# Splitting the second output product of three tiles into two token halves, and turning batch 6's keys earlier

## The chip, the cores and the metric

The kernel runs on one core of a Trainium2 chip. The engines of the core work side by side, each through its own instructions in order: TensorE (PE, with its weight loads shown apart as PEld), VectorE (DVE), ScalarE (ACT), GpSimd (POOL) and SyncE (SP, which here only issues transfers). What one engine needs of another it waits for on semaphores. The metric is the device time of one execution in microseconds. It was 226.36 us before the change, the median of 3 runs.

## The reference

Attention with keys and values pooled eight to one, followed by a feed-forward layer whose hidden value is the largest of three linear maps. Cut to what is computed:

```python
# q, k, v: (8 batches, 8 heads, 576 tokens, 64)
k_p = k.reshape(B, H, 72, 8, D).mean(axis=3)
v_p = v.reshape(B, H, 72, 8, D).mean(axis=3)
attn = softmax(q @ k_p.T / 8)
x = (attn @ v_p)               # as 4608 tokens x 512
h = max(x @ w1, x @ w2, x @ w3)      # 4608 x 768
out = h @ w_out                # 4608 x 512
```

## The kernel before

The 4608 tokens are worked through as nine tiles of 512. Tile n has a hidden stage (`hidden`, the maximum of the three maps) and an output stage. The maximum of three is taken as x @ w1 plus max(0, x @ (w2 - w1), x @ (w3 - w1)), and the x @ w1 part is folded into the output: the output of a tile is x @ (w1 @ w_out) + h' @ w_out, a product over ten rows of 128 (four of x, six of h').

A batch has 576 tokens, a tile 512. So the attention of the batches runs beside the tiles, one batch ahead: while tile n is in its stages, batch n+1 is scored (`s0` to `s7`, one head each), then its five chunks of 128 tokens are summed over the values (`v0` to `v4`) and turned into the layout that the tiles read (`x0` to `x4`, transposes that SP issues as DMAs).

For tiles 2, 3 and 4 the output stage is seven products in place of eight: a two by two split of the matrix product by a scheme with seven multiplications (`out_seven`, `PRODUCTS`). Each of the seven works on 256 tokens (two halves of 128, called m = 0 and 1) by 256 output columns, with five row blocks r for each half: ten matmuls. The line that does them is L715. The products go into three PSUM banks: 1, 6, 5 and 3 into oA, 2 into oB, and 7 and then 4 into oC. The banks of these tiles come from two groups: oA has a tag `tr` with one buffer, so that each of its four products waits until the one before is copied out; oB and oC come from the tag `pw` with three buffers, which the hidden stages' products use too. `evict` takes the results out: ACT copies oA into an output buffer (L725), DVE adds oB or oC to it (L728). Product 2's bank is added to the half of the output that 1 and 6 wrote; oC is added to the upper columns of the other half when 5 and 7 are done, and after product 4 to the upper columns of the first half. Then SP stores each half.

In these tiles the order on every engine is written out by hand, as a list of steps (`MIDDLE`). `middle(n)` walks through that list and records each step's instructions, and the engines keep that order. A digit is a product; `v2 x2` are chunk 2's value sums, its normalization and its transpose; `7:T` is the transpose of batch 7's queries; `6:k` is the key turn of batch 6.

The value sums of a chunk are 8 matmuls (L270) into a buffer of the tag `att`, which has two and gives them in rotation. DVE then takes the reciprocal of the row sums (L276) and multiplies (L278); the multiply is the last reader of that buffer. The scores (`psc`, L220) and the key turn use the same two buffers.

The key turn (`turn_k`) is three transposes on PE (L201) of the pooled keys `kp` into a PSUM tile `pkt`, and four copies out of it into the key matrices `kz` (L210): two by DVE, then two by ACT. Scores of a batch read both matrices. In tiles 2 to 4 the turn of the batch that is to be scored stands in the hidden stage, behind its first product. Batch 6 is scored from the start of tile 5's hidden stage on, and its turn stands at the end of tile 4's output stage.

The hidden products of a tile are L364 (`pw`), their relu on ACT is L370, their maximum on DVE L372; the exponentials of the scores are L225 on ACT.

Of the kernel before, what the change touches and what calls it, by code (L numbers as in the profile page):

```python
# [14 lines left out]
def kernel(  # L15
# [46 lines left out]
    def psum(shape, dtype, name, tag, bufs):  # L62
        return pools[-1].tile(shape, dtype, name=name, tag=tag, bufs=bufs)
# [86 lines left out]
    def tokens(t0, t1, k0=0, k1=KCH):  # L150

        t0, t1 = t0 % RING, (t1 - 1) % RING + 1
        assert t0 < t1
        return xT[:, k0:k1, t0:t1]
# [244 lines left out]
    def new_two():  # L399
        return sb3.tile([128, 2, C], F32, name="osb", tag="osb", bufs=3)  # L400
# [160 lines left out]
    def turns(n):  # L561
        return (pad3 if n % 2 else pad)[:, 0:4]
# [17 lines left out]
    def out_w(z, r0, r1):  # L580

        i, j = divmod(z, 2)
        c = slice(HALF * i, HALF * i + HALF)
        return (wm_sb[:, 2 * j + r0:2 * j + r1, c] if r1 <= 2
                else wo_sb[:, JH * j + r0 - 2:JH * j + r1 - 2, c])

    def out_s(z):
        return so_new[0][:, z - 1]
# [56 lines left out]
    def out_seven(n):  # L645

        mid = len(pools) < 3
        if mid:
            o = {}
        else:  # L650
            o = sb2.tile([128, 2304], F32, name="ob", tag="et")[:, 0:2048].rearrange(
                "p (j m c) -> p j m c", j=2, m=2)
            o = [o[:, 0], o[:, 1]]
        lo, hi = slice(0, HALF), slice(HALF, C)
        banks, done = {}, set()

        def store(e, j, c):
            for u in range(2):
                b, g = divmod(2 * (4 * n + 2 * j) + u, NG)
                pair = g + 2 < NG and GS[g + 2] == GS[g] + 4  # L660
                for m in range(0, 2, 1 + pair):
                    b, g = divmod(2 * (4 * n + 2 * j + m) + u, NG)
                    dst = out[S * b:S * b + S, :].rearrange("(r g) c -> r g c", g=NG)
                    e.dma_start(out=dst[:, GS[g]:GS[g] + 4 * pair + 1:4, c],
                                in_=o[j][64 * u:64 * u + 64, m:m + 1 + pair, c])

        def bank(of, m):
            if n < LAST:
                if of not in banks:
                    if mid:  # L670
                        tag = TR if of == "A" else PW
                        banks[of] = psum([128, 2, HALF], F32, name=f"o{of}", tag=tag[0],
                                         bufs=tag[1])
                    elif of == "A":
                        banks["A"] = psum([128, 2, 2, HALF], F32, name="oA", tag="val",
                                          bufs=1)[:, 0]
                    else:
                        tag = (PO, SC)[of == "C"]
                        banks[of] = psum([128, 2, HALF], F32, name=f"o{of}", tag=tag[0],
                                         bufs=tag[1])  # L680
                return banks[of]
            if (of, m) not in banks:
                tag = {"A": PA, "B": SC, "C": BC if m == 0 else SC}[of]
                banks[of, m] = psum([128, 2, HALF], F32, name=f"o{of}", tag=tag[0],
                                    bufs=tag[1])[:, 0:1]
            return banks[of, m]

        def product(i, *ms):
            if mid:
                for r in range(5):  # L690
                    for m in ms:
                        matmuls(i, m, (r,))
            else:
                for m in ms:
                    matmuls(i, m)
            done.update((i, m) for m in ms)
            evict(i, ms)

        def matmuls(i, m, rows=range(5)):
            of = "B" if i == 2 else "C" if i in (4, 7) else "A"  # L700
            p = bank(of, m)[:, m if n < LAST else 0]
            za, zb = PRODUCTS[i]
            for r in rows:
                c = slice(128 * m, 128 * m + 128)
                if isinstance(zb, str):
                    z = int(zb[1]) - 1
                    left = (tt_all[0][:, z, r, c] if mid else
                            turns(n)[:, z, r, c] if r < 2 else th[n][z][:, r - 2, c])
                else:
                    at = HALF * (zb % 2) + 128 * m  # L710
                    left = (tokens(NB * n + at, NB * n + at + 128)[:, 2 * (zb // 2) + r] if r < 2
                            else hTs[n][:, JH * (zb // 2) + r - 2, at:at + 128])
                right = (out_s(int(za[1]))[:, r] if isinstance(za, str)
                         else out_w(za, r, r + 1)[:, 0])
                nc.tensor.matmul(  # L715
                    p, left, right, stop=(r == 4), skip_group_check=True,
                    start=(i in FIRST and r == 0 and (m == 0 or n == LAST)))

        def evict(i, ms):
            m, at = ms[0], slice(ms[0], ms[-1] + 1)  # L720

            def copy(j, c):
                if j not in range(len(o)):
                    o[j] = new_two()
                nc.scalar.copy(out=o[j][:, at, c], in_=bank("A", m))  # L725

            def plus(j, c, of):
                nc.vector.tensor_tensor(out=o[j][:, at, c], in0=o[j][:, at, c],  # L728
                                        in1=bank(of, m), op=ALU.add)

            def ended(*parts):
                return all((z, k) in done for z in parts for k in range(2))

            if i in (1, 5, 6, 3):
                copy(int(i in (5, 3)), lo if i in (1, 3) else hi)
            elif i == 2:
                plus(0, lo, "B")
            elif i == 4:
                plus(0, hi, "C")
            if i in (5, 7) and (12 - i, m) in done:  # L740
                plus(1, hi, "C")
            if n == LAST and i in (5, 7) and ended(5, 7):
                store(nc.sync, 1, hi)
            if n == LAST and i == 3 and ended(3):
                store(nc.scalar, 1, lo)
            if n < LAST and i in (5, 7, 3) and ended(5, 7, 3):
                store(nc.sync, 1, slice(0, C))
            if n == LAST and i in (2, 4) and ended(i):
                store((nc.gpsimd, nc.sync)[i // 4], 0, (lo, hi)[i // 4])
            if n < LAST and i in (2, 4) and ended(2, 4):  # L750
                store(nc.sync, 0, slice(0, C))

        return product
# [102 lines left out]
    def weave():  # L856

        products, seen = {}, {}
        for name in ORDER.split():
# [29 lines left out]
        2: """  # L889
            h k k5< q5< v5< h a1 a3 a2 a4 S S ! v3+2 h h s0 h s1 h s2 h s3 h s4 b1 f f ! k4+1 h s5  # L890
            h s6 h s7 h b2 b3 b4 ! k4+2 v4+1
            1 v0 x0 2 v1 x1 6 7 v2 x2 5:T 5 v3 x3 v4 x4 3 4
        """,
        3: """
            h k k6< q6< v6< h a1 a3 a2 a4 f ! v4+2 h h s0 h s1 h s2 h s3 h s4 b1 f ! k5+1 h s5
            h s6 h s7 h b2 b3 b4 ! k5+2 v5+1
            1 v0 x0 2 v1 x1 6:T 6 7 v2 x2 5 v3 x3 v4 x4 3 4
        """,
        4: """
            h k k7< q7< v7< h a1 a3 a2 a4 f ! v5+2 h h s0 h s1 h s2 h s3 h s4 b1 f ! k6+1 h s5  # L900
            h s6 h s7 h b2 b3 b4 f ! k6+2 v6+1
            1 v0 x0 2 v1 x1 7:T 6 7 v2 x2 5 v3 x3 v4 x4 3 6:k 4 v6+2 k7+3 v7+3
        """}
    folds = iter([f for wi in range(1, 3) for f in [fold_w(wi)] * 4])

    def middle(n):

        pieces, outs, out_tiles = hidden(n), None, project(n)
        for name in MIDDLE[n].split():
            if name == "h":  # L910
                next(pieces)
            elif name == "F":
                next(out_tiles)
            elif name == "f":
                next(next(folds))
            elif name == "!":
                held[:] = gate
            elif name.isdigit():
                outs = outs or out_seven(n)
                outs(int(name), 0, 1)  # L920
            elif name[0] in "ab":
                sums_of(n, name)
            elif name[2:3] in ("<", "+"):
                pool_step(n, name)
            else:
                b, _, step = name.rpartition(":")
                do(int(b or n + 1), step)
        assert next(pieces, None) is None

    tt_all.append(const.tile([128, 4, 5, HALF], F16, name="tt", tag="tt"))  # L930
    for n in range(1, 5):
        middle(n)
# [12 lines left out]
    outs = out_seven(LAST)  # L945
# [36 lines left out]
```

## Time and profile before

| | us |
|---|---|
| runs before the change | 226.1, 226.36, 226.71 |
| profiled execution, time | 226.65 |
| profiled execution, span from first to last instruction | 224.9 |
| PE busy | 215.5 (96%) |
| DVE busy | 149.1 (66%) |
| POOL busy | 140.1 (62%) |
| ACT busy | 122.2 (54%) |
| output stage of tile 2 | 89.90 to 99.16 |
| output stage of tile 3 | 111.61 to 120.87 |
| output stage of tile 4, with the key turn | 133.32 to 143.29 |

How to read it: the profile is one execution, its times are microseconds from the first instruction. A row of the timeline gives start, duration, engine, line, operation, the tile written and the tiles read, the shape, the number of instructions merged into the row, and in brackets how long the engine had been idle before it and whom it waited for. The duration of a matmul row reaches to a modelled end and overlaps the next row, so that the time a group of matmuls costs PE is the distance between starts. The difference between the time of an execution and its span lies before the first and behind the last instruction.

### The profile page before, as it was taken

How to read it: one execution, taken by the hardware profiler on the slowest of the kernel's cores; microseconds unless marked ns; L12 is line 12 of the kernel's file. 1: busy time of each engine (PE TensorE's matmuls, PEld its weight loads, DVE VectorE, ACT ScalarE, POOL GpSimd, SP SyncE). 2: the span in 40 equal slices, each digit the busy share in tenths (PEclk: the TensorE clock that was granted, in tenths of full speed). 3: DMA queues.
4: the chain of work that ended last, by engine and by line, in shares of the span. 5: the costliest groups of instructions: out<-in, count | busy, mean ns of one | idle time of the engine just before them, and what ended most of it. 6: DMA issues, size and time to landing. Idle time of an engine off the chain costs nothing.

```text
span 224.9 us, 4690 instructions
## 1 busy us (share of the span) xinstructions
PE 215.5 (96%) x1806; PEld 146.9 (65%) x1807; DVE 149.1 (66%) x292; ACT 122.2 (54%) x221; POOL 140.1 (62%) x111
## 2 busy tenths in 40 slices
PE   7888999999999999999999999899999999999993
PEld 2477745558656545975596568555677777788882
DVE  4668876037594395877588668636677786898840
ACT  2277524755874578238724862484786446555330
POOL 7984300999949977787768757999600903772020
PEclk9999999999999999999999999999999999999999
DMA  6999999989749999659999998764341534200266
GB/s 176 210 196 197 204 208 205 206 151 236 137 105 174 233 200 224 121 108 159 244 202 158 161 261 140 153 155 92 71 95 36 122 63 89 47 3 0 60 201 163
DMA packets 50710, 33.54 MB, mean 149 GB/s; under 512 B 27040, under 2 KB 46368, under 8 KB 50688
## 3 DMA queue, kind: packets, MB, share of 16 engines
q0 software_dynamic: 20304, 16.98, 48.1%
q1 hardware_dynamic: 29936, 15.87, 31.9%
q10 hardware_dynamic: 448, 0.39, 0.7%
q8 instruction: 14, 0.23, 0.4%
q14 instruction: 8, 0.07, 0.1%
HBM read 34.60 MB, written 9.44 MB: 196 GB/s over the span
## 4 chain that ended last, share of the span: by engine, by line
PE 71%; DMA 12%; POOL 11%; issue 2%; DVE 1%; ACT 1%; POOLq 0%; ACTq 0%
PE pw L364 21%; PE oA L715 9%; DMA vt<-in_v_dram 8%; PE pA L791 7%; PE po L418 7%; PE po L414 5%; PE psc L220 4%; PE oC L715 4%; DMA mw<-in_moe_w_dram 4%; PE pC L791 3%; POOL half L163 3%; PE pav L270 3%; PE oB L715 2%; POOL half L164 2%; PE pB L791 2%
## 5 line engine op out<-in xcount | busy, mean ns | idle before, releaser
L364 PE MATMUL pw<-xT,mw 128*128 128x512 f16 (+1 forms) x336 | 72.8, 348 | 0.3 <-ACT xT L264 0.2
L364 PEld LDWEIGHTS <-mw 128*128 128x128 f16 x336 | 31.7, 98 | 20.4 <-issue 0.6
L372 DVE TENSOR_TENSOR hT<-t,pw 128x512 f16<-128x512 f16 (+1 forms) x42 | 25.4, 609 | 23.9 <-ACT et L225 14.9
L225 ACT ACTIVATE et<-psc 72x576 f16<-72x576 f32 (+2 forms) x54 | 35.2, 661 | 6.7 <-PE psc L220 6.6
L163 POOL TENSOR_TENSOR half<-vt 72x2048 f32<-72x2048 f16 x7 | 28.4, 4058 | 13.8 <-DMA vt<-in_v_dram 13.3
L164 POOL TENSOR_TENSOR half<-half 72x1024 f32<-72x1024 f32 (+1 forms) x13 | 27.3, 2098 | 10.7 <-DVE rcp L276 6.1
L370 ACT ACTIVATE t<-pw 128x512 f16<-128x512 f32 (+1 forms) x42 | 22.5, 537 | 14.8 <-PE pw L364 14.3
L278 DVE TENSOR_TENSOR xn<-pav,rcp 128x512 f16<-128x512 f32 x40 | 27.7, 691 | 1.4
L220 PE MATMUL psc<-qT,kz 128*128 128x320 bf16 (+2 forms) x120 | 22.6, 278 | 1.3 <-DVE qT L196 0.9
L418 PE MATMUL po<-mwo,hT 128*128 128x512 f16 (+1 forms) x102 | 23.5, 366 | 0.0
L220 PEld LDWEIGHTS <-kz 128*128 128x128 bf16 x143 | 13.1, 98 | 13.8 <-ACT qT L196 1.1
L163 POOL TENSOR_TENSOR half<-ktFalse 96x1536 f32<-96x1536 f16 x6 | 18.8, 3129 | 4.0 <-issue 2.9
L797 ACT CAST pad<-pA 128x512 f16<-128x512 f32 x27 | 15.6, 588 | 7.2 <-PE pA L791 7.0
L566 POOL TENSOR_TENSOR pad<-xT 128x256 f16<-128x256 f16 x8 | 6.0, 752 | 21.2 <-ACT pad L797 12.6
L270 PEld LDWEIGHTS <-et 72*128 72x128 f16 x320 | 15.2, 98 | 3.5 <-issue 0.2
L725 ACT COPY osb<-oA 128x512 f32<-128x512 f32 x12 | 7.0, 586 | 19.2 <-PE oA L715 19.2
L276 DVE RECIPROCAL rcp<-pav 128x8 f32<-128x8 f32 x40 | 8.1, 203 | 13.8 <-PE pav L270 13.3
L414 PE MATMUL po<-wm,xT 128*128 128x512 f16 (+1 forms) x68 | 16.6, 366 | 0.0
L270 PE MATMUL pav<-vp,et 72*128 72x65 f16 x320 | 16.4, 194 | 0.1
L423 ACT COPY osb<-po 128x512 f32<-128x512 f32 (+1 forms) x16 | 9.2, 573 | 12.0 <-PE po L418 12.0
L791 PEld LDWEIGHTS <-sw 128*128 128x128 f16 x144 | 13.7, 98 | 2.5
L768 DVE TENSOR_TENSOR pad<-pad,pC 128x512 f16<-128x512 f16 x18 | 12.3, 685 | 3.9 <-PE pC L791 3.6
(122 smaller groups left out, 383.2 us busy)
## 6 DMA issues: line engine op xcount, KB each, us to landing
out_dram<-osb SPq DMA_DIRECT2D x38, 128.0 KB, 5.3
ktFalse<-in_k_dram POOLq DMA_DIRECT2D x7, 576.0 KB, 8.3
qb<-in_q_dram POOLq DMA_DIRECT2D x7, 576.0 KB, 11.6
vt<-in_v_dram POOLq DMA_DIRECT2D x7, 576.0 KB, 16.8
mw<-in_moe_w_dram POOLq DMA_DIRECT2D x9, 256.0 KB, 9.3
out_dram<-osb SPq DMA_DIRECT2D x8, 256.0 KB, 5.7
ktTrue<-in_k_dram SPq DMA_DIRECT2D x3, 384.0 KB, 5.1
out_dram<-ob SPq DMA_DIRECT2D x8, 128.0 KB, 2.6
```

The costliest lines, as they stand in the source:

```text
L163: yield e.tensor_tensor(out=f, in0=t[:, :, 0:4, :], in1=t[:, :, 4:8, :], op=ALU.add)
L164: yield e.tensor_tensor(out=f[:, :, 0:2, :], in0=f[:, :, 0:2, :], in1=f[:, :, 2:4, :], op=ALU.add)
L220: nc.tensor.matmul(out, kz_all[b % 2][f % 2][rows, h, :], qTs[b][rows, n + i0:n + i1, 64 * (h % 2):64 * (h % 2) + 64], start=True, stop=True)
L225: nc.scalar.activation(out=out, in_=in_, func=FT.Exp, scale=1.0 / 64.0)
L270: nc.tensor.matmul(pav[:, h // 4, 65 * (h % 4):65 * (h % 4) + 65], ets[b][:, h, c0:c0 + 128], vp_all[:, b, h, :], start=True, stop=True)
L278: nc.vector.tensor_tensor(out=xn, in0=pv[:, :, :, 0:D], in1=rcp.to_broadcast([128, 2, 4, D]), op=ALU.mult)
L364: mm = nc.tensor.matmul(pw, w_sb[wi][:, kc, bass.ts(jc, 128)], x[:, kc], start=(kc == 0), stop=(kc == KCH - 1))
L372: nc.vector.tensor_tensor(out=hT[:, jc, c0:c1], in0=t, in1=pw, op=ALU.max)
L414: nc.tensor.matmul(po, tokens(128 * m, 128 * m + 128)[:, kc], wm_sb[:, kc, c], start=(kc == 0), stop=False)
L418: nc.tensor.matmul(po, hT[:, jc, bass.ts(mm, 128)], wo_sb[:, jc, c], start=False, stop=(jc == JCH - 1))
L715: nc.tensor.matmul(p, left, right, stop=(r == 4), skip_group_check=True, start=(i in FIRST and r == 0 and (m == 0 or n == LAST)))
L791: mm = nc.tensor.matmul(p[:, w], a[:, kc, bass.ts(g, 128)], b[:, kc, :], start=(i in FIRST and w + kc == 0), stop=(w + kc == 2), skip_grou ...
```

## The change

Two parts. Product 2 of tiles 2, 3 and 4 can now be written as two steps, `2l` (m = 0) and `2h` (m = 1), each with five matmuls, and its bank is added only when both are done. In tiles 2 and 3 the first half stays where product 2 stood and the second goes between `v3` and `v4`. In tile 4 the first half stands behind `v1`, the second behind `v4`, and the key turn of batch 6 stands behind that, ahead of products 3 and 4 (before, between 3 and 4). In the built program the number of instructions on each engine's work stays the same.

```diff
@@ out_seven, product
                 for m in ms:
                     matmuls(i, m)
             done.update((i, m) for m in ms)
-            evict(i, ms)
+            if not mid:
+                evict(i, ms)
+            elif (i, 1) in done:
+                evict(i, (0, 1))
@@ MIDDLE, tile 2
-            1 v0 x0 2 v1 x1 6 7 v2 x2 5:T 5 v3 x3 v4 x4 3 4
+            1 v0 x0 2l v1 x1 6 7 v2 x2 5:T 5 v3 x3 2h v4 x4 3 4
@@ MIDDLE, tile 3
-            1 v0 x0 2 v1 x1 6:T 6 7 v2 x2 5 v3 x3 v4 x4 3 4
+            1 v0 x0 2l v1 x1 6:T 6 7 v2 x2 5 v3 x3 2h v4 x4 3 4
@@ MIDDLE, tile 4
-            1 v0 x0 2 v1 x1 7:T 6 7 v2 x2 5 v3 x3 v4 x4 3 6:k 4 v6+2 k7+3 v7+3
+            1 v0 x0 v1 x1 2l 7:T 6 7 v2 x2 5 v3 x3 v4 x4 2h 6:k 3 4 v6+2 k7+3 v7+3
@@ middle
+            elif name in ("2l", "2h"):
+                outs = outs or out_seven(n)
+                outs(2, "lh".index(name[1]))
```

A step "2l" calls the same function with one half in place of two. In `MIDDLE`, the steps behind `4` in tile 4 are sums that POOL makes of the values of batches 6 and 7 and the keys of batch 7.

## The prediction

> **What bounds the kernel now.** I read the page first (busy times, slices), then the waits of TensorE from the first middle tile on, then the timeline of the three output stages.
>
> ```profile
> span 224.9 us, 4690 instructions
> PE 215.5 (96%) x1806; PEld 146.9 (65%) x1807; DVE 149.1 (66%) x292; ACT 122.2 (54%) x221; POOL 140.1 (62%) x111
> PEclk9999999999999999999999999999999999999999
> ```
>
> ```profile
> 145.00:221.00 76.00, 76.00 (x647) 57.08 (x644) 53.37 (x92) 43.07 (x81) 35.66 (x34) 1.00 0.36 83
> ```
>
> TensorE (PE) is busy for 96% of the span, and the row of one stretch, 145 to 221 us (columns: length, then PE, PEld, DVE, ACT, POOL), shows it busy for all 76.00 us. So whatever moves PE's position at 145 us should move the end by as much: from there on no wait for another engine is left on PE. The change lies before that point, where the output stages of tiles 2, 3 and 4 start at 89.90, 111.61 and 133.32. I name the steps as the kernel does: v0 to v4 are the value sums of the five token chunks, 1 to 7 the products. Tile 2:
>
> ```profile
> 90.99 0.42 PE L270 MATMUL pav<-vp,et 72*128 72x65 f16 x8
> 91.25 0.60 PE L715 MATMUL oB<-wm,xT 128*128 128x256 f16 x4
> ...
> 95.05 1.25 PE L715 MATMUL oA<-so,tt 128*128 128x256 f16 x10
> 96.15 0.68 PE L270 MATMUL pav<-vp,et 72*128 72x65 f16 x16
> 96.35 0.59 ACT L725 COPY osb<-oA 128x512 f32<-128x512 f32 x1 [1.86 <-PE oA L715]
> 96.96 0.69 DVE L728 TENSOR_TENSOR osb<-osb,oC 128x512 f32<-128x512 f32 x1 [0.78 <-ACT osb L725]
> 96.98 0.60 PE L715 MATMUL oA<-so,xT 128*128 128x256 f16 x4 [0.15 <-ACT osb L725]
> 98.07 0.60 PE L715 MATMUL oC<-wm,tt 128*128 128x256 f16 x4
> 99.16 1.03 PE L364 MATMUL pw<-xT,mw 128*128 128x512 f16 x4
> ```
>
> Matmuls overlap, so a price on PE is the distance between two starts. One v (8 matmuls) costs 91.25 - 90.99 = 0.26 us, a whole product (10 matmuls) 98.07 - 96.98 = 1.09. Products 5 and 3 share the one bank oA: 3 cannot start before ACT has copied 5 out (96.35 to 96.94). Between them stand only v3 and v4, which fill 96.15 to 96.15 + 2 x 0.26 = 96.67. So PE idles 96.98 - 96.67 = 0.31 us (the row says 0.15, because it counts from the modelled end of the last matmul). Tile 3 is a copy of it, 117.86 + 0.52 = 118.38 against 118.69, again 0.31:
>
> ```profile
> 117.86 0.68 PE L270 MATMUL pav<-vp,et 72*128 72x65 f16 x16
> ...
> 118.69 0.60 PE L715 MATMUL oA<-so,xT 128*128 128x256 f16 x4 [0.16 <-ACT osb L725]
> ```
>
> Tile 4 has three gaps. First PE and ACT, then DVE:
>
> ```profile
> 133.32 0.60 PE L715 MATMUL oA<-wm,xT 128*128 128x256 f16 x4
> ...
> 134.62 0.59 ACT L725 COPY osb<-oA 128x512 f32<-128x512 f32 x1 [1.07 <-PE oA L715]
> ...
> 138.49 1.26 PE L715 MATMUL oA<-so,tt 128*128 128x256 f16 x10
> 139.58 0.69 PE L270 MATMUL pav<-vp,et 72*128 72x65 f16 x16
> 139.78 0.59 ACT L725 COPY osb<-oA 128x512 f32<-128x512 f32 x1 [1.86 <-PE oA L715]
> 140.41 0.60 PE L715 MATMUL oA<-so,xT 128*128 128x256 f16 x4 [0.15 <-ACT osb L725]
> 142.07 0.29 PE L201 MATMUL pkt<-ident,kp 96*128 96x96 bf16 x3 [0.41 <-DVE rcp L276]
> 142.20 0.60 PE L715 MATMUL oC<-wm,tt 128*128 128x256 f16 x4
> 143.29 1.03 PE L364 MATMUL pw<-xT,mw 128*128 128x512 f16 x4
> 143.74 0.96 ACT L210 COPY kz<-pkt 64x288 bf16<-64x288 bf16 x2 [1.45 <-DVE kz L210]
> 144.15 0.30 PE L220 MATMUL psc<-qT,kz 128*128 128x320 bf16 x1
> 144.73 0.60 ACT L370 ACTIVATE t<-pw 128x512 f16<-128x512 f32 x1
> 144.76 0.28 PE L220 MATMUL psc<-qT,kz 128*128 128x256 bf16 x1 [0.31 <-ACT kz L210]
> 144.88 1.03 PE L364 MATMUL pw<-xT,mw 128*128 128x512 f16 x4
> 145.22 0.64 ACT L225 ACTIVATE et<-psc 72x576 f16<-72x576 f32 x1
> ...
> 146.85 0.41 PE L220 MATMUL psc<-qT,kz 128*128 128x320 bf16 x2
> ```
>
> ```profile
> 140.40 0.69 DVE L728 TENSOR_TENSOR osb<-osb,oC 128x512 f32<-128x512 f32 x1 [0.78 <-ACT osb L725]
> 141.00 0.20 DVE L276 RECIPROCAL rcp<-pav 128x8 f32<-128x8 f32 x1
> 141.23 0.69 DVE L278 TENSOR_TENSOR xn<-pav,rcp 128x512 f16<-128x512 f32 x1
> 141.84 0.20 DVE L276 RECIPROCAL rcp<-pav 128x8 f32<-128x8 f32 x1
> 142.07 0.69 DVE L278 TENSOR_TENSOR xn<-pav,rcp 128x512 f16<-128x512 f32 x1
> 142.68 0.97 DVE L210 COPY kz<-pkt 64x288 bf16<-64x288 bf16 x2
> 143.68 0.69 DVE L728 TENSOR_TENSOR osb<-osb,oC 128x512 f32<-128x512 f32 x1
> ```
>
> Gap one is the same 0.31 before 3 (140.10 to 140.41). Gap two stands before the key turn: 3 ends at 140.41 + 1.09 = 141.50, the turn starts at 142.07, 0.57 later. Its tile takes one of two rotating buffers, the one that v3's sums held, and chunk 3's multiply (141.23 to 141.92) is their last reader. Gap three is in the first score of batch 6: its second matmul waits for ACT's copies of the keys, which come after DVE's; 144.76 - 144.15, less the 0.13 that a 320-column matmul takes at the rate of 0.109 for 256, is 0.48.
>
> **The change part by part.** No matmul, copy or DMA is added or removed. 2 becomes two halves of 5 matmuls, 0.545 us each, of which one goes behind v3 (tiles 2, 3) or behind v4 (tile 4); the addition of its bank (oB) moves with the second half; in tile 4 v1 goes ahead of the first half, and the key turn with its four key copies ahead of 3. A split product costs no more per matmul: neighbouring matmuls of the present 1.09 already start 0.109 apart, and a change between v and product costs nothing beyond 0.26 (the 16 of two v's and the 8 of one cost the same each).
>
> *Tiles 2 and 3.* Everything from the first half to v3 comes 0.545 earlier on PE. Product 5 starts at 95.05 - 0.545 = 94.50; its copy ends 1.89 after that start, at 96.40. PE now has v3, the second half and v4 behind 5: 94.50 + 1.09 + 0.26 + 0.545 + 0.26 = 96.66. So 3 finds its bank free, with 0.23 to spare, and starts at 96.66 instead of 96.98: **-0.31 each, -0.63 for both** (unrounded starts). Were the cover gone, the price is the gap again; the bounds are 0 and -0.31 per tile.
> What else could wait: 6 now follows its predecessor sooner, by 0.545 (before, 1.09 + 2 x 0.26 lay between 1's end and 6, now 0.545 + 0.52); 1's copy ends 135.21 - 133.32 = 1.89 after 1's start, 6 comes 1.09 + 0.52 + 0.545 = 2.16 after it. DVE gets its 0.69 addition late, between chunk 3 and chunk 4, but its queue there starts 0.545 earlier (the addition of oC waits for 5's copy, 96.96 - 0.545 = 96.41), so DVE ends level with before while PE is 0.31 ahead; the bank oB is needed again by the next tile's second hidden product, at about 98.84 + 0.86 + 0.13 = 99.83, where that addition ends at 96.41 + 0.61 + 0.23 + 0.61 + 0.69 = 98.55 (distances as in the DVE rows of tile 4 below). SP's transposes keep their order; chunk 1's goes out sooner.
>
> *Tile 4.* 1, v0, v1, first half, 6, 7, v2: 5 starts at 138.49 - 0.545 = 137.945 (locally, as if nothing had been gained before). Its copy ends at 139.83. DVE, in order, does the oC addition first (138.49 to 140.40 is 1.91, so at 139.855), then chunk 3: the multiply ends at 139.855 + (141.92 - 140.40) = 141.375, and the turn can start at 139.855 + (142.07 - 140.40) = 141.525. But PE reaches it at 137.945 + 1.09 + 0.52 + 0.545 = 140.10. **The turn waits 1.42**, and 3 and 4, which nothing holds any more (5's copy was out at 139.83), queue behind it. Turn 0.13, 3 and 4 at 1.09 each: the next tile's first product starts at 143.83 instead of 143.29, **+0.54**.
> Then it pays back. DVE: chunk 4's multiply at 141.525, the oB addition 0.61 later, the key copies 0.61 later still, at 142.745; ACT's start 1.06 after DVE's (143.74 - 142.68), at 143.805, and release the score 1.02 later (144.76 - 143.74), at 144.825. The score's first half starts at 143.83 + 0.86 = 144.69 and lasts 0.13, so gap three is gone, and the next product starts at 144.94 against 144.88: **tile 4 in all +0.06**. The stall has eaten gaps one, two and three, 0.31 + 0.57 + 0.48 = 1.36 against 1.42. Bounds: -1.36 if nothing holds the turn up, +0.90 if it waits for chunk 4's multiply (rivals).
> ACT gets later: the key copies end at 143.805 + 0.96 = 144.77, 3's copy (0.59) now stands behind them, the relu follows at 145.36, the first exponential 0.49 after it (145.22 - 144.73), so that it ends at 146.49 instead of 145.86. The third score needs that buffer at 146.85 + 0.06, so 0.4 is left; were that cover gone, the price is what ACT is late, 0.63 at most. 3's store goes out behind SP's last transpose as before.
>
> **The sum.** -0.63 + 0.06 = -0.57. The profiled execution took 226.65 (span 224.9 and 1.75 around it): 226.08. That execution lies 0.29 above the median shown, 226.36, against which I forecast **225.8**, -0.25%.
>
> **The rivals.**
> *The turn is covered* (224.4). If the bank that the turn takes were free by 140.10, all of tile 4's 1.36 would go too: 226.36 - 0.63 - 1.36. For it: the kp sums are long there, POOL is not named. Against: the chunk 3 multiply follows 5's copy in DVE's order, and that cannot end by then.
> *The turn waits for chunk 4* (226.6, slower than before). For it: the row names a reciprocal as releaser, and the one at 141.84 is chunk 4's. Then the turn would start 0.84 later (142.07 - 141.23), the next tile's second product at 145.78, +0.90: 226.36 - 0.63 + 0.90. It decides as soon as the buffer in turn is v4's. Against: before the change the turn started at 142.07, when chunk 4's multiply only began.
> *The gaps of tiles 2 and 3 stay* (226.4), the change not doing what it says there: v4 or 3 held by DVE's later queue, so that only tile 4's +0.06 is left. Against: 0.23 of room, worked out above.
> *The stall costs matmul speed* (228.0). TensorE works at half rate here, at its start, which the granted-clock row does not show:
>
> ```profile
> 1.53 4.45 PE L436 MATMUL wm<-warm 128*128 128x512 bf16 x10 [1.53 <-DVE warm L117]
> ...
> 11.09 0.60 PE L220 MATMUL psc<-qT,kz 128*128 128x256 bf16 x4 [0.86 <-DVE qT L196]
> ```
>
> Ten matmuls of 512 columns take 4.45, 0.42 from start to start, against 0.217 in the rows of pw (four in 1.03). If 1.42 us of idling brought that rate back for as long as this row, 4.45 us, half of that is lost: 225.8 + 2.2. It decides from an idle stretch between 0.86, after which four score matmuls of 256 columns run at full rate (0.60 in all), and 1.42. Nothing in the rows excludes it.
> [...]
>
> **How the numbers follow.** Forecast 0.62, turn covered 0.09, turn waits for chunk 4 0.11, gaps stay 0.10, half rate 0.08. The forecast's own range, 225.4 to 226.2, comes from the scatter of the runs shown (226.1 to 226.71) and 0.2 of rounding in the working. A measurement of this kernel tells about 0.3%, 0.68 us, from no change; the forecast straddles that bound (225.68), with 0.30 of its 0.62 below. Faster 0.30 + 0.09 and a little of scatter: 0.40. Slower: the half rate, and 0.06 from the upper ends of the two middle rivals, 0.14. Same 0.46. The range 225.2 to 226.7 leaves out the covered turn and the half rate.
>
> **What would show it.** In the profile after: in tiles 2 and 3 product 3 directly behind v4 with no wait named; the first pw row of the next tile 0.31 and 0.63 earlier (98.84, 120.24); in tile 4 an idle stretch of about 1.4 before L201, with DVE named, 3 and 4 behind it without waits, no gap inside the first score, and L364's second product at about 144.3; 3's copy on ACT behind the key copies. Wrong would be: a wait before 3 or before v4 in tiles 2 and 3, L201 waiting well under 1 or over 2 us, a new wait of PE for ACT's exponentials near 146, or matmuls of 0.42 behind the stall.

## The result, and the profile after

| | before | after |
|---|---|---|
| median of 14 runs each, same chip, us | 226.78 | 226.38 |
| lowest and highest | 226.1, 227.35 | 225.9, 227.08 |
| profiled execution: time, span | 226.65, 224.9 | 226.51, 224.8 |

The ratio is 0.9983, with a 95% interval of 0.9975 to 0.9992: the changed kernel is 0.4 us faster (0.18 to 0.57), inside the 0.3% that the prediction called no change. The forecast was -0.57 us, at the end of that interval. The level of the kernel before also lay 0.42 us above the three runs that the forecast of 225.8 was set against, so of the 0.58 between 225.8 and 226.38, 0.42 is the level and some 0.17 the change.

The page after the change (span, busy time of each engine) gives nothing away:

```profile
span 224.8 us, 4685 instructions
PE 215.1 (96%) x1806; PEld 146.6 (65%) x1807; DVE 149.4 (66%) x292; ACT 122.0 (54%) x221; POOL 139.8 (62%) x111
```

The view of TensorE's waits from 60 to 221 us (who waited, for whom; total, times, longest) has three rows in the kernel before, and one after the change:

```profile
PE oA L715 <- ACT osb L725: 0.5, 3, 0.2
PE pkt L201 <- DVE rcp L276: 0.4, 1, 0.4
PE psc L220 <- ACT kz L210: 0.3, 1, 0.3
```

```profile
PE pkt L201 <- DVE rcp L276: 1.3, 1, 1.3
```

In the changed kernel L718 is the line of the products that was L715, L728 ACT's copy of oA (was L725), L731 DVE's addition (was L728).

The timeline of tile 2's output stage, and the three rows of tile 3 that answer to it (start, duration, engine, line, operation; rows that say nothing here are left out):

```profile
90.05 0.60 PE L718 MATMUL oA<-wm,xT 128*128 128x256 f16 x4
...
94.67 1.25 PE L718 MATMUL oA<-so,tt 128*128 128x256 f16 x10
95.76 0.42 PE L270 MATMUL pav<-vp,et 72*128 72x65 f16 x8
95.96 0.58 ACT L728 COPY osb<-oA 128x512 f32<-128x512 f32 x1 [1.86 <-PE oA L718]
96.02 0.38 PE L718 MATMUL oB<-wm,xT 128*128 128x256 f16 x2
96.24 0.49 PE L718 MATMUL oB<-mwo,hT 128*128 128x256 f16 x3
96.56 0.43 PE L270 MATMUL pav<-vp,et 72*128 72x65 f16 x8
96.83 0.60 PE L718 MATMUL oA<-so,xT 128*128 128x256 f16 x4
98.02 0.68 DVE L731 TENSOR_TENSOR osb<-osb,oB 128x512 f32<-128x512 f32 x1
99.01 1.03 PE L364 MATMUL pw<-xT,mw 128*128 128x512 f16 x4
...
117.97 0.42 PE L270 MATMUL pav<-vp,et 72*128 72x65 f16 x8
118.23 0.60 PE L718 MATMUL oA<-so,xT 128*128 128x256 f16 x4
...
120.41 1.03 PE L364 MATMUL pw<-xT,mw 128*128 128x512 f16 x4
```

Product 3 now stands 0.27 behind v4 (96.56 to 96.83; one v costs 0.26) with no wait named: 5's copy was out at 95.96 + 0.58 = 96.54, 0.29 early. The stage lasts 99.01 - 90.05 = 8.96 instead of 9.26. From there to the first hidden product of the next tile are 120.41 - 99.01 = 21.40 us, before 120.87 - 99.16 = 21.71. Tile 4:

```profile
132.87 0.60 PE L718 MATMUL oA<-wm,xT 128*128 128x256 f16 x4
...
141.06 0.29 PE L201 MATMUL pkt<-ident,kp 96*128 96x96 bf16 x3 [1.26 <-DVE rcp L276]
141.19 0.60 PE L718 MATMUL oA<-so,xT 128*128 128x256 f16 x4
142.27 0.97 DVE L210 COPY kz<-pkt 64x288 bf16<-64x288 bf16 x2
142.28 0.60 PE L718 MATMUL oC<-wm,tt 128*128 128x256 f16 x4
143.37 1.03 PE L364 MATMUL pw<-xT,mw 128*128 128x512 f16 x4
143.60 0.97 ACT L210 COPY kz<-pkt 64x288 bf16<-64x288 bf16 x2 [4.25 <-PE oC L718]
144.24 0.68 PE L220 MATMUL psc<-qT,kz 128*128 128x320 bf16 x2
144.62 0.10 PEld L220 LDWEIGHTS <-kz 128*128 128x128 bf16 x1 [0.51 <-ACT kz L210]
144.75 1.03 PE L364 MATMUL pw<-xT,mw 128*128 128x512 f16 x4
```

The turn starts 141.06 - 132.87 = 8.19 behind the stage's start, after 1.43 us without matmuls, and the next tile's first product 143.37 - 132.87 = 10.50 behind it. But the first score takes 0.68, where its two matmuls take 0.41 further on in both profiles: its second one still waits 0.27 for ACT's key copies. The weights of that matmul are keys, and their load (PEld, 144.62) is released by these copies, which end at 143.60 + 0.97. They start 1.33 behind DVE's (143.60 - 142.27), before 1.06, and 0.36 behind the end of DVE's (142.27 + 0.97 = 143.24), before 0.09 (142.68 + 0.97 = 143.65 against 143.74). The second product stands 144.75 - 132.87 = 11.88 behind the stage's start, before 11.56: +0.32 for tile 4, in place of +0.06. The three stages together: -0.30 - 0.31 + 0.32 = -0.29. In the two profiles 0.15 of it does not show, because this execution reached tile 2's output stage 0.15 later (90.05 against 89.90), ahead of anything that was changed there; from the second product on both take the same to the last matmul (75.99 us before, 75.95 after, from start to start).

Two things are left to find out: why ACT's copies are late, and what a turn without the stall would be worth.

### The profile page after: what moved, and what is told of

It is laid out like the page before. It is cut to its first block, busy times and chain, and to the rows that moved or that the text cites. A ratio compares the mean times of both kernels' runs of the same rounds, so it can differ in the third digit from the quotient of the medians.

```text
span 224.8 us, 4685 instructions
## 1 busy us (share of the span) xinstructions
PE 215.1 (96%) x1806; PEld 146.6 (65%) x1807; DVE 149.4 (66%) x292; ACT 122.0 (54%) x221; POOL 139.8 (62%) x111
## 4 chain that ended last, share of the span: by engine, by line
PE 71%; DMA 12%; POOL 11%; issue 2%; DVE 1%; ACT 1%; POOLq 0%
PE pw L364 21%; PE oA L718 10%; DMA vt<-in_v_dram 8%; PE pA L794 7%; PE po L418 7%; PE oC L718 5%; PE po L414 5%; PE psc L220 4%; DMA mw<-in_moe_w_dram 4%; PE pC L794 3%; PE pav L270 3%; POOL half L163 3%; PE oB L718 2%; POOL half L164 2%; PE pB L794 2%
## 5 line engine op out<-in xcount | busy, mean ns | idle before, releaser
L164 POOL TENSOR_TENSOR half<-half 72x1024 f32<-72x1024 f32 (+1 forms) x13 | 27.3, 2098 | 10.7 <-DVE rcp L276 6.1
L728 ACT COPY osb<-oA 128x512 f32<-128x512 f32 x12 | 7.0, 585 | 16.7 <-PE oA L718 16.7
L774 DVE SCALAR_TENSOR_TENSOR hT<-pad 128x512 f16<-128x512 f16 x18 | 14.1, 797 | 2.3 <-ACT pad L804 1.9
```

What stands on the lines that cost most here:

```text
L164: yield e.tensor_tensor(out=f[:, :, 0:2, :], in0=f[:, :, 0:2, :], in1=f[:, :, 2:4, :], op=ALU.add)
```

## Experiments

The ratios are to the kernel before, run on the same chip in the same rounds, with a 95% interval; they are not the quotient of the two medians, from which they differ by up to 0.001. The step lists are those of `MIDDLE`.

**One part at a time.** t23 has the halves in tiles 2 and 3 alone, t4 the change of tile 4 alone, turnback the whole change but with the key turn back between 3 and 4.

```diff
@@ t23, tile 4
+            1 v0 x0 2 v1 x1 7:T 6 7 v2 x2 5 v3 x3 v4 x4 3 6:k 4 v6+2 k7+3 v7+3
@@ t4, tiles 2 and 3
+            1 v0 x0 2 v1 x1 6 7 v2 x2 5:T 5 v3 x3 v4 x4 3 4
+            1 v0 x0 2 v1 x1 6:T 6 7 v2 x2 5 v3 x3 v4 x4 3 4
@@ turnback, tile 4
+            1 v0 x0 v1 x1 2l 7:T 6 7 v2 x2 5 v3 x3 v4 x4 2h 3 6:k 4 v6+2 k7+3 v7+3
```

> Split in tiles 2 and 3 alone, tile 4 as before the change. If the two gaps before product 3 are worth what the profile after shows (0.30 and 0.31 us) and tile 4 gives half of it back: 0.61 us faster than before, ratio 0.9973, 0.23 to 0.3 us faster than the whole change. If tile 4 is neutral, as the prediction had it: the same time as the whole change, ratio 0.9983.

> Tile 4's part alone, tiles 2 and 3 as before the change. By the profile after: 0.32 us slower than before, ratio 1.0014, with the stall of 1.43 before the key turn and 0.26 inside the first score. By the prediction: 0.06 slower, ratio 1.0003. If the late copies of ACT were an accident of one execution, the gap inside the first score is near 0 here.

> The whole change, but with the key turn back between products 3 and 4. The DVE chain that the score waits for stays: the turn waits 0.33 behind 3, ACT's key copies start 0.04 behind their wait (3's copy stands ahead of them again), and the second product of the next tile comes as the prediction had it, 0.57 us ahead of before: ratio 0.9975. If ACT's lateness came from its long idle time or from product 4, it shows here too or not at all; if the key turn's place is what costs, 0.26 us less than the whole change.

t23: 226.16 against 226.47, ratio 0.9979 (0.9966 to 0.9991); its two stages last 8.96 and 8.95, and tile 4's second product stands 11.55 behind the stage's start as before. t4: 226.90, ratio 1.0010 (0.9996 to 1.0025), +0.10% that the interval cannot tell from nothing; its stages 2 and 3 last 9.27 and 9.26, and tile 4 comes to 145.45 - 133.56 = 11.89. turnback: 226.18, ratio 0.9979 (0.9967 to 0.9992), tile 4 at 144.08 - 132.49 = 11.59. So the gain is that of tiles 2 and 3: the forecast -0.63, -0.28%, lies in t23's interval. That tile 4's part gives some of it back is read from the rows (11.89 against 11.55); the times of t23, turnback and the whole change have intervals that overlap. Rows of tile 4, first t4, then turnback:

```profile
142.96 0.98 DVE L210 COPY kz<-pkt 64x288 bf16<-64x288 bf16 x2
144.30 0.97 ACT L210 COPY kz<-pkt 64x288 bf16<-64x288 bf16 x2 [4.26 <-PE oC L718]
```

```profile
140.69 0.29 PE L201 MATMUL pkt<-ident,kp 96*128 96x96 bf16 x3 [0.17 <-DVE rcp L276]
141.89 0.96 DVE L210 COPY kz<-pkt 64x288 bf16<-64x288 bf16 x2
142.94 0.96 ACT L210 COPY kz<-pkt 64x288 bf16<-64x288 bf16 x2 [1.81 <-PE pw L364]
143.96 0.28 PE L220 MATMUL psc<-qT,kz 128*128 128x256 bf16 x1 [0.74 <-ACT kz L210]
```

In t4 the copies again start 1.34 behind DVE's, so this was no accident of one execution; in turnback 1.05. Back behind 3, the turn hardly waits, and the idle time stands in the first score instead: the same DVE queue ends both.

**Why ACT's copies are late.** In the built program ACT waits for DVE's copies in an instruction of its own, just ahead of its first copy, and that copy itself waits for the turn's transposes; neither waits for product 4, which the bracket names. In the trace the wait for DVE is over at 143.27, 0.03 behind the end of DVE's copies, and the copy starts at 143.60: the time is lost between the two. Three theories: (1) the place in the program: the first of them is ACT's 193rd instruction in the changed kernel and in t4, counted from the start of the program with all of its instructions (before the change 3's copy stood ahead of it, and it was the 194th), and ACT loses time at that place; (2) a hidden wait for the end of product 4; (3) ACT starts slowly after more than 4 us without work. Three one-column copies on ACT, ahead of tile 4's product 1 where ACT has time, move the copies to another place in the program and leave the waits as they are: by (1) the key copies are then in time, by (2) and (3) as late as before. After_pad writes them into a new tile, after_pad2 into a column of a tile that the kernel has:

```diff
@@ middle
+            elif name == "p":
+                for _ in range(3):
+                    nc.scalar.copy(out=warm[:, 1:2], in_=warm[:, 0:1])
@@ MIDDLE, tile 4 (after_pad: out=spare, with the line below)
+            p 1 v0 x0 v1 x1 2l 7:T 6 7 v2 x2 5 v3 x3 v4 x4 2h 6:k 3 4 v6+2 k7+3 v7+3
+    spare = const.tile([128, 1], BF16, name="spare", tag="spare")
```

> The whole change, with three one-column copies more on ACT just ahead of tile 4's first product, where ACT is idle for 1.07 us. [...] Theory 2, the key copies wait for product 4's end, and theory 3, ACT starts late after more than 4 us of idling: nothing changes, 0.26 stays.

> As after_pad, but the three copies write a column of a tile that is there already, so that no buffer moves. [...] Theories 2 and 3 (product 4's end, long idling): a gap of 0.26 as in the change itself, 0.9983.

After_pad2 ran in 225.98 against 226.79, ratio 0.9968 (0.9954 to 0.9982). Its key copies:

```profile
142.33 0.96 DVE L210 COPY kz<-pkt 64x288 bf16<-64x288 bf16 x2
143.38 0.97 ACT L210 COPY kz<-pkt 64x288 bf16<-64x288 bf16 x2 [3.97 <-DVE kz L210]
```

ACT starts 1.05 behind DVE again, the score has no gap, and tile 4 takes 144.54 - 132.92 = 11.62, the 11.62 of the forecast (144.94 - 133.32). The key copies have kept their waits and their idle time (3.97 us) and have changed their place in the program, so the delay hangs on the place. Two more pairs of kernels that differ only in the three copies say the same: 0.36 to 0.37 behind DVE's end without them, some 0.09 with them, in shift32 and after_pad and in early and early_pad2 (all below). The times alone would not show it: the intervals of after_pad2 and of the whole change overlap. Why this place costs time is not shown. Against (2) and (3) speaks the next kernel, early, too: there ACT's copies are late by as much (0.37 behind DVE's end), after 2.81 us of idling and with product 4 over (it starts at 140.12 and costs 1.09, to 141.21; the copies start at 141.61).

After_pad has its copies in time as well, but ran in 232.32. Its 14 executions scatter from 226.56 to 234.91; the four shortest, up to 229.5, give a ratio of 1.0028 (0.9997 to 1.0059), which is not clear of no change. In the profiled one, of 233.18, TensorE stood still ahead of tile 3's hidden stage:

```profile
103.86 1.86 PE L364 MATMUL pw<-xT,mw 128*128 128x512 f16 x4 [5.03 <-DMA xT<-xn]
```

```profile
104.00:108.00 4.00, 4.00 (x13) 1.52 (x12) 1.17 (x3) 1.53 (x3) 1.96 (x3) 0.50 0.90 160
```

The second row is a stretch (length, then the engines' busy times, granted clock, DMA share, GB/s): behind a stall of 5 us the granted clock is 0.50 from 104 to 108 us, and the four matmuls of the first row take 1.86 instead of 1.03. In the built program the new tile had moved later buffers by 32 bytes. Shift32 is the changed kernel with that tile and without the copies:

```diff
+    spare = const.tile([128, 1], BF16, name="spare", tag="spare")
```

> The whole change with an unused tile of one column, which moves the buffers allocated behind it by 32 bytes, and no copies. If that move is what made after_pad slow and not its three copies: loads land late again (the 576 KB loads of tile 2 some 15 to 22 us after their issue instead of 8 to 13), PE waits several us for a transpose ahead of tile 3, and the time is 227 to 235. If it was the copies: 226.4.

Its two runs (229.5 and 230.8) have a median of 230.15, ratio 1.0152 (1.0114 to 1.019): a stall comes without the copies too, 2.9 us, also ahead of tile 3's hidden stage. With two runs, and after_pad's scatter, the size of the effect is uncertain. What moved is seen in the DMA view from 78 to 104 us (transfer, queue, count, KB each, median us from issue to landing), first the changed kernel, then shift32:

```profile
ktFalse<-in_k_dram POOLq DMA_DIRECT2D x2, 576.0 KB, 8.1
qb<-in_q_dram POOLq DMA_DIRECT2D x2, 576.0 KB, 11.4
vt<-in_v_dram POOLq DMA_DIRECT2D x2, 576.0 KB, 15.1
...
xT<-xn SPq DMA_TRANSPOSE x6, 2.4
```

```profile
ktFalse<-in_k_dram POOLq DMA_DIRECT2D x2, 576.0 KB, 10.1
qb<-in_q_dram POOLq DMA_DIRECT2D x1, 576.0 KB, 15.8
vt<-in_v_dram POOLq DMA_DIRECT2D x1, 576.0 KB, 19.6
...
xT<-xn SPq DMA_TRANSPOSE x5, 4.8
```

The medians mix the loads of two tiles. Taken one by one, the loads issued at 79 to 81 us land later, the queries 15.8 us behind their issue instead of 10.7 and the values 19.6 instead of 13.4, and the transposes that the hidden stage needs land twice as late among them (4.8 against 2.4). The next ones, issued at 100 to 105 us into buffers that have moved by the same 32 bytes, hold nothing up: from tile 3's first hidden product to tile 5's shift32 takes 146.30 - 101.94 = 44.36 us, the changed kernel 143.37 - 99.01 = 44.36. So the move does not bring a stall with every set of loads, and why it made these late stays open. In the same kernel ACT's copies are late once more (DVE's end at 145.20 + 0.96, ACT's start at 146.52): their place in the program is that of the changed kernel.

**A turn without the stall.** The turn waited for the buffer of v3's sums, that is for chunk 3's multiply, because v4 stood ahead of it. In early it stands right behind v3 and takes the other buffer, v2's; the second half of 2, 3 and 4 follow, and v4 comes last. Early_pad2 adds the three copies to that.

```diff
@@ early, tile 4 (early_pad2: with p ahead of 1)
+            1 v0 x0 v1 x1 2l 7:T 6 7 v2 x2 5 v3 x3 6:k 2h 3 4 v4 x4 v6+2 k7+3 v7+3
```

> Tile 4 reordered behind product 5: v3, key turn, second half, 3, 4, v4. If the stall is the turn's buffer, held by v3 until DVE has done 5's addition and chunk 3, it goes away when the turn takes the buffer before (v2's), and the key copies come ahead of the oB addition and of chunk 4: tile 4 to the second product of the next tile 10.49 us against 11.55 before and 11.88 in the change; with 0.61 from tiles 2 and 3 1.67 us faster than before, ratio 0.9926. ACT's first key copy is the 193rd instruction here too: some 0.3 late, a gap of about 0.17 inside the first score. If the stall comes from something else (the pooled keys, the copies), the turn waits here as well, and the ratio stays above 0.996.

> The same with the three copies of one column on ACT ahead of tile 4's first product. Theory 1: key copies 0.04 behind their wait, the gap inside the first score gone, 0.16 us less than without them, ratio 0.9919. Theory 2 or 3: as without them.

Early: 225.33 against 226.79, ratio 0.9946 (0.9927 to 0.9964). Tile 4, and then the place in tile 6 where a new wait stands:

```profile
132.31 0.60 PE L718 MATMUL oA<-wm,xT 128*128 128x256 f16 x4
...
138.01 0.43 PE L270 MATMUL pav<-vp,et 72*128 72x65 f16 x8
138.34 0.30 PE L201 MATMUL pkt<-ident,kp 96*128 96x96 bf16 x3
...
140.12 0.60 PE L718 MATMUL oC<-wm,tt 128*128 128x256 f16 x4
140.27 0.97 DVE L210 COPY kz<-pkt 64x288 bf16<-64x288 bf16 x2
141.61 0.96 ACT L210 COPY kz<-pkt 64x288 bf16<-64x288 bf16 x2 [2.81 <-PE oC L718]
142.87 1.02 PE L364 MATMUL pw<-xT,mw 128*128 128x512 f16 x4
...
158.96 1.33 POOL L166 TENSOR_TENSOR vp<-half 72x512 f16<-72x512 f32 x1
159.20 1.38 DVE L566 TENSOR_TENSOR pad<-xT,pad 128x512 f16<-128x512 f16 x1
160.63 0.60 PE L794 MATMUL pA<-pad,sw 128*128 128x256 f16 x4 [0.48 <-DVE pad L566]
```

The stall is gone (the turn 0.33 behind v3, which costs 0.26), and tile 4 takes 142.87 - 132.31 = 10.56, 1.32 less than after the change (10.49 was expected). But the changed kernel has these rows in tile 6:

```profile
159.55 1.27 POOL L166 TENSOR_TENSOR vp<-half 72x512 f16<-72x512 f32 x1
161.14 0.42 DVE L566 TENSOR_TENSOR pad<-xT,pad 128x512 f16<-128x512 f16 x1
```

DVE's second subtraction there takes 1.38 in place of 0.42: in early it starts while POOL's last sum of a batch's values runs, and ends only after that. PE is ahead of the changed kernel by about 1.9 us there (132.87 - 132.31 = 0.56 from the start of tile 4's output stage, 1.32 in it), POOL only by 159.55 - 158.96 = 0.59, so that DVE's work behind PE meets POOL's, and PE waits 0.64 in all. Early_pad2 came out at 225.53, ratio 0.9941 (0.9920 to 0.9962), and, run again on another chip as early_pad2b, at 225.73 against 226.53, 0.9968 (0.9956 to 0.9980). Its score has no gap, tile 4 takes 143.26 - 132.98 = 10.28, and the wait in tile 6 is 0.90: the 0.28 that the copies save in tile 4 is lost there again. The last kernel lets POOL's sums begin earlier: a subtraction of DVE, which stands ahead of the step that POOL waits for, moves forward in tile 4's list:

```diff
@@ early3, tile 4, hidden stage
-            ... s4 b1 f ! k6+1 h s5 ... b4 f ! k6+2 v6+1
+            ... s4 b1 f f ! k6+1 h s5 ... b4 ! k6+2 v6+1
```

> The same kernel as early_pad2, to compare with early3 on one chip: ratio 0.994.

> early_pad2 with one subtraction of DVE (a 128x768 step of the folded weights) taken from tile 4's output stage to its hidden stage, beside the one that stands there. POOL's last 25 us of work begin behind that subtraction, without a pause, and end with the sum at which the fp16 subtraction of tile 6 waited (0.9 us lost ahead of product pA). If POOL's sums hold that subtraction, they end 0.5 us earlier here and the wait falls to about 0.4: 0.5 us less than early_pad2, ratio 0.992. If it is something else of the subtraction, 0.9 stays.

Early3: 225.49 against 226.53, ratio 0.9949 (0.9933 to 0.9966); that it lies below early_pad2b on the same chip is not clear of noise, as the intervals overlap. POOL's sum of the keys starts at

```profile
135.08 1.81 POOL L164 TENSOR_TENSOR half<-half 96x768 f32<-96x768 f32 x1 [1.50 <-DVE rcp L276]
...
158.64 1.40 POOL L166 TENSOR_TENSOR vp<-half 72x512 f16<-72x512 f32 x1
158.94 1.37 DVE L566 TENSOR_TENSOR pad<-xT,pad 128x512 f16<-128x512 f16 x1
```

where early_pad2b has it at 135.76, its stage starting 0.35 later; so POOL gained about 0.3. The wait in tile 6 shrank from 0.92 to 0.64, half of what was expected. All of these beat the kernel before. Early and early3 also lie clear of the changed kernel (0.9975 to 0.9992), the second run of early_pad2 does not. That this wait is all that is left to gain was not tried.

## Why the prediction was half right

- *Tiles 2 and 3, "-0.31 each"*: right, -0.30 and -0.31, with the room at 3's bank 0.29 (forecast 0.23). DVE's later addition held nothing up. t23 shows the two alone at -0.21% (-0.09 to -0.34).
- *"The turn waits 1.42"*: right, 1.43, and its start 8.19 behind the stage's start against 141.525 - 133.32 = 8.205. *"+0.54"* for the next tile's first product: right, 10.50 against 143.83 - 133.32 = 10.51. Which buffer is in turn, and who reads it last, was read off correctly; the rival in which the turn waits for chunk 4 would have had it 0.84 later, and early, where the other buffer is in turn, has no stall.
- *DVE's key copies at 142.745*, 9.425 behind the start: 142.27 - 132.87 = 9.40, right.
- *"ACT's start 1.06 after DVE's (143.74 - 142.68), at 143.805"*: this is the step that failed. Measured 1.33. With it *"gap three is gone"* was wrong, 0.27 of it stayed, and *"tile 4 in all +0.06"* became +0.32. The distance was taken from a row in which ACT was free to go on at once; the 193rd place of its program, which the reordering gave to just this copy, costs 0.28 (1.33 against 1.05 behind DVE's start). Shown by after_pad2, where three idle copies give the 1.05 and the 11.62 back; with them the rows of the three stages come to -0.30 - 0.31 + 0.06 = -0.55, against the forecast's -0.57. Why that place costs it stays open.
- *"against which I forecast 225.8"*: the level of 226.36, from three runs, was 0.42 too low, as 14 runs have 226.78. That part of the miss is no step of the mechanism.
- *The exponentials of ACT, 0.4 of cover*: held, though ACT was later than worked out; PE names no wait near 146.
- *The rivals*: the turn was not covered; it did not wait for chunk 4; no gap of tiles 2 and 3 stayed; and 1.43 us of idling brought no half rate back (product 3's first four matmuls take 0.60 right behind the turn, as before the change).

The sum of the forecast with tile 4 as measured is -0.63 + 0.32 = -0.31, which lies in the measured interval of -0.18 to -0.57.

## What to carry to other kernels

A step that is moved takes its waits with it, and these can be worked out row by row; but a distance between two engines that is read off one place holds only while neither loses time of its own. Where a row starts some tenths behind the release that the program gives it, and the profile names an unlikely releaser, look at what number the instruction has on its engine (here the 193rd on ACT, 0.36 to 0.37 behind the release in place of some 0.09): a few idle instructions ahead of it, where the engine has time, show whether the place in the program costs the time. And whatever makes PE earlier makes it meet what did not become earlier: here the sums of POOL, 20 us behind the change, took back about half of the 1.3 us that a better place of the turn gave.

## What the runs showed of the hardware

- ACT starts the copy that is instruction 193 of its program 0.36 to 0.37 behind the end of DVE's copies (the changed kernel, t4, early, shift32), and 0.08 to 0.09 behind where it has another number (before, turnback, after_pad, after_pad2, early_pad2). Three pairs of kernels that differ only in three idle copies ahead of it tie it to the place in the program. Why that place costs time was not shown.
- Buffers that lie 32 bytes further on cost 1.5% in the two runs of shift32. One set of 576 KB loads lands 5.1 (queries) and 6.2 us (values) later; the next set, moved by 32 bytes as well, brought no stall (44.36 us from tile 3's first hidden product to tile 5's, with the move and without it). So the move alone does not explain the late ones, and their cause was not shown.
- Behind a stall of 1.43 us product 3's first four matmuls took 0.60, as before the change, and behind one of 2.9 us in shift32 four hidden matmuls took 1.02, at a granted clock of 1.00: full rate both times. Behind one of 5 us in after_pad four hidden matmuls took 1.86, and the granted clock was 0.50 for the 4 us from 104 to 108.
- A subtraction on DVE of two tiles (`xT` and `pad`) took 1.38 in early against 0.42 in the changed kernel, beside a sum on POOL that had started 0.24 earlier, and ended 0.29 after it. The kernel before and the changed one show it too, on the first subtraction of tile 6, where PE had time: it overlaps the sum by 0.49 and 0.19 and ends 0.28 and 0.29 behind it, after 0.77 and 0.48.
